# Two heads on one core: the first phase recorded, ordered by a list scheduler in the kernel, and its first keys loaded early

## The chip, the cores and the metric

The kernel runs on one core of a Trainium2 chip. The metric is the device time of one execution in microseconds (us). The engines are PE (TensorE, matrix products), DVE (VectorE), ACT (ScalarE), POOL (GpSimd) and SP (SyncE, which here only issues DMAs). Each takes its instructions in a fixed order; semaphores hold an instruction until what it reads is there and what it overwrites is free.

## The reference

Two independent heads share the sequence of 2048 positions; their outputs of 448 columns each are put side by side. Inputs and outputs are float32.

```python
# head A: a diagonal state-space convolution, 448 channels, 256 states each
dt = exp(log_dt); A = -exp(log_A_real) + 1j * A_imag; C = (C_real + 1j * C_imag) * dt[:, None]
P = exp((A * dt[:, None])[:, :, None] * pos)
K = 2.0 * einsum("dn,dnl->dl", C, P).real
y = irfft(rfft(u_t, 2 * L) * rfft(K, 2 * L))[:, :, :L]
a = y + u * D_skip
# head B: full attention, 16 heads of 28
q, k, v = split(x @ wqkv)
p = softmax(einsum("bhqd,bhkd->bhqk", q, k) * 28 ** -0.5)
b = einsum("bhqk,bhkd->bhqd", p, v) @ wo
out = concatenate([a, b], axis=-1)
```

## The kernel before

**Phases.** `body` has a first phase (the block `with ExitStack() as st:`) and a main loop behind it. The first phase computes queries, keys and values, the *seeds* (the exponentials from which the main loop multiplies up the powers of head A), and the largest scores of the first attention unit. The main loop runs over 16 units (4 groups of 4 heads by 4 chunks of 512 queries) of 16 key tiles each, and mixes scores, exponentials, products with v, the maxima of the next unit and head A's convolution by a written list of slots. Only the first phase is changed.

**Projections.** x comes in four chunks of 512 positions (`load_x`, tile `xn`), is transposed on PE and split into a high and a low part (`xh`, `xl`). `qk_proj(c, s, g)` multiplies chunk c with the weights of group g (s = 1 for keys, 0 for queries): 12 matmuls of 512 columns into a PSUM bank `pm`; ACT and DVE evict it into `hl`, and SP stores it to DRAM (`k_d`, `q_d`). `v_proj` does the values with 12 matmuls of 448 columns; they go to `v_d`. For half of the keys a difference is stored as well (`dhl`, `kd_d`). That makes 48 jobs in the list `work`; in the last chunk the four value jobs stand ahead of the eight others.

**Seeds.** `seeds(o)` handles one of eight octets of channels: loads (`nat`), scales on ACT, transposes into `pn`, phases and sizes in the large tile `tri`, sines and exponentials on ACT (which needs another function table for each kind), products on POOL and DVE (`qhat` as a workspace, `sg`, `px`), and two stores into `sd_d`. The octets are interleaved with the projections in steps: octet o starts its stages at step `SP * o`, and `PW = 37` steps hold the 48 projection jobs.

**First maxima.** Softmax needs an upper bound of each row's scores. For unit 0 it is found at the end of the first phase: 16 groups (4 heads by 4 tiles of 128 queries) of five matmuls. The maximum of two blocks of scores is built as relu(a - b) + b: a product of the query with the key difference `kdif` (or with one quarter of the keys, less another, by means of the negated queries `nq`) goes through ACT's relu into `rl`, and one DVE instruction adds b and reduces. Both halves of a group share tiles of two banks, so there are 16 relus of 1024 columns and 16 reductions of 1024. `max_end` transposes the 16 columns and `max_put` writes the negated maxima `mh` into two rows of the queries `qhat`, by a DMA on ACT's queue. Only then can the main loop's scores `pss` start.

**Places.** The keys of group 0 lie in `k0_t`. The same memory holds the split weights of the projections until these are done:

```python
        w_g = k0_t[:CK].rearrange("p g (i s k h e) -> p i s k g h e", i=2, s=2, k=NCK, h=HG)
```

so the key loads, written at the steps `KW = (33, 35, 36)` and behind step `PW`, wait for the last projection that reads the weights of that head. The maxima have their own pools (`m_p`, `ps_2`), opened when the projections' pools are closed.

**Order.** `KEPT["p"] = ()` leaves the first phase to the framework's own scheduler, which sets the order of instructions on each engine when the kernel is built; `KEPT["a"]` keeps the main loop's engines in the order of the program. `project` emits an eviction one job later than its matmuls.

Of the kernel before, what the change touches and what calls it, by code (L numbers as in the profile page):

```python
# [8 lines left out]
F32 = mybir.dt.float32  # L9
F32R = mybir.dt.float32r  # L10
# [7 lines left out]
L = 2048  # L18
# [25 lines left out]
A0, A1, KW = 26, 34, (33, 35, 36)  # L44
# [21 lines left out]
class Kept:  # L66
# [5 lines left out]
    def __getattr__(self, name):  # L72
        f = getattr(self.engine, name)

        def call(*args, **kw):
            i = f(*args, **kw)  # L76
            return self.owner.tc.keep_in_program_order(i) if self.name in self.owner.kept else i
        return call


class Engines:
    def __init__(self, tc):
        self.tc, self.kept = tc, ()
        for n in ("tensor", "vector", "scalar", "gpsimd", "sync"):
            setattr(self, n, Kept(self, n, getattr(tc.nc, n)))


KEPT = {"p": (), "a": ("tensor", "vector", "scalar", "gpsimd", "sync"), "f": ()}
# [3 lines left out]
def body(ctx, tc, a, out):  # L92
# [41 lines left out]
    k0_p = pool(k0_st, "k0_p", side="right")  # L134
    k0_t = k0_p.tile([128, HG, L], F32R, name="khat")
# [10 lines left out]
    def load_k(g, j, p):  # L146
        if j == 0:
            t = k0_t if g == 0 else p.tile([128, HG, L], F32R, name="khat")
            kt_g[g] = [t[:, i] for i in range(HG)]
        for r in range(4):  # L150
            nc.sync.dma_start(kt_g[g][j][32 * r:32 * r + 32, :].bitcast(F32), k_d[g][r % 2, 32 * j:32 * j + 32, :])
# [47 lines left out]
    def max_end(u, ps):  # L199
        nc.tensor.transpose(ps[:16, :128], m_u[u, 1], ident)  # L200
        mh = q_p.tile([16, 2, 128], F32R, name="mh")
        nc.vector.tensor_scalar(mh[:, 0, :], ps[:16, :128], -1.0, None, op0=ALU.mult)
        nc.vector.scalar_tensor_tensor(mh[:, 1, :], ps[:16, :128], -1.0, mh[:, 0, :].bitcast(F32),
                                       op0=ALU.mult, op1=ALU.subtract)
        mh_u[u] = mh
# [7 lines left out]
    with ExitStack() as st:  # L213
        sst, xst, wst, mst, psx, psm = (ExitStack() for _ in range(6))
# [3 lines left out]
        y_p = pool(wst, "y_p", side="right")  # L218
        ps_w[0] = pool(psx, "ps_w", 1, PSUM)
# [3 lines left out]

        xns = {}

        def load_x(c):
            xs = x[c * CQ:(c + 1) * CQ, :].rearrange("(t p) d -> p t d", p=128)
            for h in range(2):
                xns[c, h] = y_p.tile([128, 2, D], F32, name="xn", bufs=3)
                nc.sync.dma_start(xns[c, h], xs[:, 2 * h:2 * h + 2, :])  # L230

        load_x(0)
        w_g = k0_t[:CK].rearrange("p g (i s k h e) -> p i s k g h e", i=2, s=2, k=NCK, h=HG)
        vh = y_p.tile([CK, NCK, D], F32R, name="vh")
        vl = y_p.tile([CK, NCK, D], F32R, name="vl")
        nc.gpsimd.memset(k0_t[:CK].rearrange("p g (n e) -> p (g n) e", e=32)[:, :, DH:].bitcast(F32), 0.0)
        vst = [v_p.tile([128, NK // NQ, HG, 32], F32, name="v", bufs=5).rearrange("p t h e -> p (t h) e") for _ in range(2)]
        for t in vst:
            nc.gpsimd.memset(t[:, :, DH:DH + 1], 1.0)
            nc.gpsimd.memset(t[:, :, DH + 1:], 0.0)  # L240
        wns = []
        for i in range(2):
            wn = t_p.tile([128, 3, LV, BO * 16], F32, name="tri", bufs=2).rearrange("p t k h -> p (t k h)")
            wn = wn[:CK, :2 * 3 * D].rearrange("p (k s d) -> p k s d", k=2, s=3)
            wns += [wn[:, 0], wn[:, 1]]
# [7 lines left out]
        def load_nat(o):  # L253
            nats[o] = s_p.tile([PO, 4, 256], F32, name="nat", bufs=2)
            for i, n in enumerate(("A_log_A_real", "A_A_imag", "A_C_real", "A_C_imag")):
                nc.sync.dma_start(nats[o][:, i, :], bass.AP(tensor=a[n].tensor, offset=a[n].offset + first(o) * 256,
                                                            ap=[[256, JF // 4], [JF * 256, 4], [1, 256]]))
# [47 lines left out]
        def turn_dt():  # L305
            dt_ps = ps_t.tile([128, CQ], F32, name="pt")[:PO, :NO]
            nc.tensor.transpose(dt_ps, dt_o, ident[:NO, :NO])
            for i, f in enumerate((1.0, 0.15915494309189535, 2.0, -2.0, -1.0)):
                nc.vector.tensor_scalar(dt_all[:, i, :], dt_ps, f, None, op0=ALU.mult)
# [4 lines left out]
        def seeds(o):  # L314
# [13 lines left out]
            def turn():  # L328
                pn = ps_n.tile([128, CQ], F32, name="pn")
                q["ps"] = ps = pn[:, :8 * PO].rearrange("p (a b h e) -> p a b h e", a=4, h=2, e=8)  # L330
                q["magic"] = pn[:, 8 * PO:8 * PO + 1]
                vec.tensor_scalar(q["magic"], half_pi, 0.0, MAGIC, op0=ALU.mult, op1=ALU.add)
                for i in range(4):
                    for h in range(2):
                        nc.tensor.transpose(ps[:, i, :, h, :], q["nat"][:, i, h * 128:(h + 1) * 128], ident[:PO, :PO])
                q["tr"] = s_p.tile([128, NH], F32, name="tr", bufs=2)
                act.activation(q["tr"], ps[:, 0].rearrange("p b h e -> p (b h e)"), AF.Copy)

            def phases():
                tri = t_p.tile([128, 3, LV, NH], F32, name="tri", bufs=2)  # L340
# [14 lines left out]
            def places():  # L355
                se = q_p.tile([128, HG, CQ], F32R, name="qhat", bufs=3).bitcast(F32).rearrange("p h q -> p (h q)")
# [5 lines left out]
            def g_place():  # L362
                q["sg"] = sg = s_p.tile([128, BO, SDF - F_G], F32, name="sg", bufs=SGB)
# [36 lines left out]
            def g_first():  # L400

                c0 = q["ps"][:, 2:4].rearrange("p c b h e -> p c (b h e)")
                px = ps_x.tile([128, CQ], F32, name="px")
# [29 lines left out]
        def transposes(c):  # L433
            for k in range(NCK):
                pt = ps_t.tile([128, CQ], F32, name="pt")[:CK]
                for t in range(4):
                    nc.tensor.transpose(pt[:, t * 128:(t + 1) * 128], xns[c, t // 2][:, t % 2, k * CK:(k + 1) * CK], ident)
                xh[k] = x_p.tile([CK, CQ], F32R, name="xh", bufs=XB)
                xl[k] = x_p.tile([CK, CQ], F32R, name="xl", bufs=XL)
# [3 lines left out]
        def qk_proj(c, s, g):  # L443
            pp = w_tile()
# [7 lines left out]
            def evac():  # L452
                hl = x_p.tile([128, 2, CQ], F32R, name="hl", bufs=2)
# [7 lines left out]
                if s == 1 and c < 2:  # L461
                    HC = CQ // 2
                    kb = y_p.tile([128, HC], F32, name="kb")
                    dhl = y_p.tile([128, 2, HC], F32R, name="dhl")
# [10 lines left out]
        def v_proj(c, t):  # L475
            pp = w_tile()
# [12 lines left out]

        work = []  # L490
        for c in range(NQ):
            jobs = [lambda c=c, s=s, g=g: qk_proj(c, s, g) for g in range(G) for s in (1, 0)]
            v_jobs = [lambda c=c, t=t: v_proj(c, t) for t in range(4)]
            jobs = v_jobs + jobs if c == NQ - 1 else jobs + v_jobs
# [11 lines left out]
        pend, n_work = [], len(work)  # L506
# [7 lines left out]
        for j, t in enumerate(KW):  # L514
            ahead[t].append(lambda j=j: load_k(0, j, k0_p))

        def project():

            e = work.pop(0)() if work else None
            while pend:  # L520
                pend.pop(0)()
            if e:
                pend.append(e)

        for t in range(n_stage):
            while work and n_work - len(work) < n_work * (t + 1) / PW:
                project()
            for f in slots[t] + ahead.get(t, []):
                f()
            if t + 1 == PW:  # L530
                project()
                wst.close()
                load_k(0, HG - 1, k0_p)
                load_q(1)
                for c in range(NQ):
                    load_v(0, c)
        xst.close()
        psx.close()
        m_p = pool(mst, "m_p")
        ps_2 = pool(psm, "ps_2", 4, PSUM)  # L540
        nq = m_p.tile([128, HG, CQ], F32R, name="nq")
        m_u[0, 1] = q_p.tile([128, HG * 4], F32, name="m1", bufs=2)
        for i in range(16):
            j, t = divmod(i, 4)
            ts = slice(t * 128, (t + 1) * 128)
            q, kt = q_u[0][:, j, ts], kt_g[0][j]
            if t == 0:
                nc.gpsimd.tensor_scalar(nq[:, j], q_u[0][:, j].bitcast(F32), -1.0, None, op0=ALU.mult)
            pd, pb = (ps_2.tile([128, 2, CQ], F32, name="p2") for _ in range(2))
            kb = kt.rearrange("p (c s n) -> p c s n", c=NQ, s=2)[:, :2, 1, :]  # L550
            mm = nc.tensor.matmul
            mm(pd[:, 0], q, kd_g[0, j], start=True, stop=True)
            mm(pd[:, 1], q, kt[:, 2 * CQ:3 * CQ], start=True, stop=False)
            mm(pd[:, 1], nq[:, j, ts], kt[:, 3 * CQ:], start=False, stop=True)
            mm(pb[:, 0].rearrange("p (c n) -> p c n", c=2), q, kb, start=True, stop=True)
            mm(pb[:, 1], q, kt[:, 3 * CQ:], start=True, stop=True)
            rl = m_p.tile([128, 2, CQ], F32, name="rl2", bufs=2)
            nc.scalar.activation(rl, pd, AF.Relu)
            nc.vector.tensor_tensor_reduce(rl, pb, rl, 1.0, -3.0e38, ALU.add, ALU.max, m_u[0, 1][:, i:i + 1])
        nc.scalar.activation(half_pi[:1], half_pi[:1], AF.Exp)  # L560
        max_end(0, ps_2.tile([128, 2, CQ], F32, name="p2")[:, 0])
        max_put(0)
        psm.close()
        mst.close()
# [12 lines left out]
    k_pools = [k0_p, kq_p]  # L577
# [580 lines left out]
```

## Time and profile before

| | |
|---|---|
| median of 3 runs | 1305.49 us (1304.11 to 1305.54) |
| profiled execution | 1307.74 us, of which the span of the trace is 1305.7 us |
| busy in the span | PE 1228.7 us (94%), ACT 980.3 (75%), DVE 907.0 (69%), POOL 865.9 (66%) |
| DMA | 205.28 MB, mean 157 GB/s |
| granted TensorE clock, mean | 0.976 |

All times below are of the one profiled execution. Busy shares are averages over phases with different limits, so they are read by stretches of time. A row of the timeline gives start, duration, engine, line, operation, target and sources, and in brackets how long the engine had been idle and what ended that. A row of a group gives the count, the busy time, the mean time of one in ns, and the idle time before them. Nearly all instructions carry line 76, the helper that passes every call on, so groups are told apart by the names of their tiles. SPq is SP issuing a DMA: its time is that of the issue, not of the transfer.

### The profile page before, as it was taken

How to read it: one execution, taken by the hardware profiler on the slowest of the kernel's cores; microseconds unless marked ns; L12 is line 12 of the kernel's file. 1: busy time of each engine (PE TensorE's matmuls, PEld its weight loads, DVE VectorE, ACT ScalarE, POOL GpSimd, SP SyncE). 2: the span in 40 equal slices, each digit the busy share in tenths (PEclk: the TensorE clock that was granted, in tenths of full speed). 3: DMA queues.
4: the chain of work that ended last, by engine and by line, in shares of the span. 5: the costliest groups of instructions: out<-in, count | busy, mean ns of one | idle time of the engine just before them, and what ended most of it. 6: DMA issues, size and time to landing. Idle time of an engine off the chain costs nothing.

```text
span 1305.7 us, 32148 instructions
## 1 busy us (share of the span) xinstructions
PE 1228.7 (94%) x12193; PEld 695.7 (53%) x12193; DVE 907.0 (69%) x2001; ACT 980.3 (75%) x2046; POOL 865.9 (66%) x684
## 2 busy tenths in 40 slices
PE   6888877799999999999999999999997999999998
PEld 5766755355555555555555555555554555545333
DVE  5676656677777787777788888888986555636111
ACT  4877875588888888888788888888886666756463
POOL 2677654478888788888769999999995221424421
PEclk9989887799999999999999999999999999999999
DMA  6677679735866455468634232743324453647666
GB/s 202 207 273 257 218 259 271 212 66 136 185 147 142 109 149 157 142 169 231 162 104 105 56 83 62 157 111 78 82 59 139 146 158 136 203 142 238 202 161 175
DMA packets 200082, 205.28 MB, mean 157 GB/s; under 512 B 95992, under 2 KB 158520, under 8 KB 197880
## 3 DMA queue, kind: packets, MB, share of 16 engines
q1 hardware_dynamic: 199864, 203.22, 56.1%
q8 instruction: 96, 1.57, 0.5%
q14 instruction: 58, 0.48, 0.1%
q10 hardware_dynamic: 64, 0.02, 0.0%
HBM read 120.74 MB, written 82.18 MB: 155 GB/s over the span
## 4 chain that ended last, share of the span: by engine, by line
PE 72%; POOL 8%; ACT 7%; DVE 5%; DMA 4%; issue 4%; SPq 0%; ACTq 0%; POOLq 0%
PE pm L76 39%; PE pss L76 16%; PE po L76 16%; POOL sg L76 2%; POOL e L76 2%; DMA khat<-k 2%; POOL tri L76 2%; ACT tri L76 1%; ACT sg L76 1%; DVE mx L76 1%; POOL p L76 1%; ACT L76 1%; ACT p L76 1%; POOL eu L76 1%; DVE rl L76 1%
## 5 line engine op out<-in xcount | busy, mean ns | idle before, releaser
L76 ACT ACTIVATE p<-pss 128x512 f32<-128x512 f32 x1024 | 560.4, 609 | 109.9 <-PE pss L76 105.9
L76 PE MATMUL pss<-qhat,khat 128*128 128x512 f32 x1024 | 405.7, 402 | 4.0 <-DMA qhat<-mh 2.2
L76 DVE TENSOR_REDUCE mx<-pm 128x1 f32<-128x512 f32 x480 | 308.3, 683 | 121.2 <-PE pm L76 119.5
L76 PE MATMUL pm<-khat,qhat 128*128 128x512 f32 x720 | 314.4, 437 | 6.1 <-ACT rl L76 3.5
L76 POOL TENSOR_TENSOR e<-e,sdb 128x256 f32<-128x256 f32 x168 | 202.0, 1203 | 108.7 <-ACT e L76 67.2
L76 PE MATMUL po<-p,v 128*32 128x512 f32 x2048 | 271.0, 597 | 0.0
L76 POOL TENSOR_TENSOR e<-e,eu 128x256 f32<-128x256 f32 x168 | 248.3, 1478 | 13.2
L76 PEld LDWEIGHTS pm<-khat,qhat 128*128 128x128 f32 x720 | 135.4, 188 | 206.4 <-ACT p L76 47.0
L76 PEld LDWEIGHTS pss<-qhat,khat 128*128 128x128 f32 x1024 | 191.2, 189 | 52.5 <-ACT p L76 13.8
L76 DVE CUSTOM_DVE_ANT_0 rl<-pm,rl 128x512 f32<-128x512 f32 x240 | 165.3, 689 | 70.0 <-ACT rl L76 67.7
L76 POOL TENSOR_TENSOR eu<-e,sdb 128x256 f32<-128x256 f32 x168 | 202.3, 1204 | 0.0
L76 POOL TENSOR_TENSOR p<-pr,pr 64x448 f32<-64x448 f32 x64 | 73.2, 1144 | 155.6 <-PE pm L76 122.3
L76 DVE TENSOR_TENSOR g<-g,zg 128x128 f32<-128x128 f32 x392 | 162.0, 413 | 3.6
L76 ACT ACTIVATE rl<-pm 128x512 f32<-128x512 f32 x240 | 145.3, 605 | 7.7 <-issue 4.1
L76 PE MATMUL pm<-xh,khat 112*128 112x512 f32 x256 | 89.7, 431 | 19.6 <-DVE hl L76 10.6
L76 PE MATMUL pm<-kdif,qhat 128*128 128x512 f32 x240 | 97.0, 404 | 1.7 <-DVE pr L76 1.1
L76 DVE TENSOR_TENSOR zg<-g,zg 128x128 f32<-128x128 f32 x224 | 88.0, 393 | 5.3
L76 PEld LDWEIGHTS pm<-e,g 128*32 128x32 f32 x3584 | 56.9, 110 | 49.2 <-issue 15.7
L76 PE MATMUL pm<-e,g 128*32 128x64 f32 x3584 | 73.6, 223 | 8.7 <-POOL e L76 8.7
L76 ACT ACTIVATE y<-pm 128x448 f32<-128x448 f32 x48 | 26.5, 553 | 59.7 <-PE pm L76 39.1
L76 PEld LDWEIGHTS pm<-xh,khat 112*128 112x128 f32 x256 | 51.0, 205 | 35.9 <-DVE hl L76 12.6
L76 DVE TENSOR_TENSOR pr<-pm,ub 128x448 f32<-128x448 f32 x64 | 37.0, 619 | 46.9 <-PE pm L76 37.7
(133 smaller groups left out, 1491.6 us busy)
## 6 DMA issues: line engine op xcount, KB each, us to landing
sdb<-sd SPq DMA_DIRECT2D x56, 336.0 KB
khat<-k SPq DMA_DIRECT2D x64, 256.0 KB
qhat<-q SPq DMA_DIRECT2D x64, 256.0 KB
sd<-sg SPq DMA_DIRECT2D x8, 1456.0 KB
k<-hl SPq DMA_DIRECT2D x16, 512.0 KB
q<-hl SPq DMA_DIRECT2D x16, 512.0 KB
v<-v SPq DMA_DIRECT2D x32, 256.0 KB
mw<-in_mw SPq DMA_DIRECT2D x16, 512.0 KB
```

The costliest lines, as they stand in the source:

```text
L76: i = f(*args, **kw)
```

## The change

Every instruction of the first phase is recorded instead of issued, with what it reads and writes. `Plan.order` gives each a duration from a table or a formula, builds the dependences from overlapping memory, and lays the instructions on five engines and one DMA resource by list scheduling: at each step the engine that is free first takes the ready instruction with the longest remaining chain. Then they are issued in that order, and all five engines are kept in it. Tiles that the framework rotated are now rings made ahead (`ring`), so that reuse is seen as a dependence.

The weights get a place of their own (`w_p`). The keys' place is opened when the chunks of x and the values' weights are done with (`change`), which needs the last value job done; the value jobs of the last chunk therefore stand second to fifth in it. From job 41 on, `first_maxima` asks for the keys of heads 2, 3, 0 and 1 and records the groups of maxima in the jobs' order (`MG`: job number to head of keys, groups). Each group is done in two halves of one bank each, from the projections' own rings: 32 relus and 32 reductions of 512 columns in place of 16 of 1024. The negated queries use the place of `nat`; three of the four `xl` tiles use the places of `v`. An eviction is recorded with its job. The differences and queries of group 0 are asked for at steps 18 and 28 (before 26 and 34); the next queries and the values are loaded through the plan.

```diff
-A0, A1, KW = 26, 34, (33, 35, 36)
+A0, A1 = 18, 28
+MG = {41: (2, ()), 42: (3, ()), 43: (0, (8, 9)), 44: (1, (10, 11)), 45: (None, (12, 13)), 46: (None, (14, 15)), 47: (None, (0, 1)),
+      48: (None, (2, 3)), 49: (None, (4, 5)), 50: (None, (6, 7))}
...
+            if self.owner.plan is not None:
+                return self.owner.plan.add(self.name, name, lambda *a_, **k_: self.owner.tc.keep_in_program_order(f(*a_, **k_)), args, kw)
...
+    def order(self):
...
+        cost = lambda o: o.span + o.wait + (2.5 + o.bytes / o.rate if o.bytes else 0.0)
+        for o in reversed(self.ops):
+            k = o.tag, o.engine
+            tail[o.i] = max([cost(o) + self.GAP + tail[j] for j in after[o.i]] + [o.span + chain.get(k, 0.0), cost(o)])
+            chain[k] = tail[o.i] if o.engine != "sync" else 0.0
...
+        while len(out) < n:
+            e = min((e for e in pools if pools[e]), key=lambda e: max(free[e], min(ready[i] for i in pools[e])))
+            t = max(free[e], min(ready[i] for i in pools[e]))
+            best = max((i for i in pools[e] if ready[i] <= t + 1e-9),
+                       key=lambda i: tail[i] * self.SCALE[self.ops[i].tag] + self.BIAS[self.ops[i].tag] - (0 if self.ops[i].table in (None, table[0]) else self.SWITCH))
...
+            if o.bytes:
+                dma[0] = max(dma[0], end + 1.3) + o.bytes / o.rate
+                end = dma[0] + 0.6
...
-KEPT = {"p": (), "a": ("tensor", "vector", "scalar", "gpsimd", "sync"), "f": ()}
+KEPT = {"p": ("tensor", "vector", "scalar", "gpsimd", "sync"), "a": ("tensor", "vector", "scalar", "gpsimd", "sync"), "f": ()}
...
-        w_g = k0_t[:CK].rearrange("p g (i s k h e) -> p i s k g h e", i=2, s=2, k=NCK, h=HG)
+        w_t = w_p.tile([CK, HG, L], F32R, name="w")
+        w_g = w_t.rearrange("p g (i s k h e) -> p i s k g h e", i=2, s=2, k=NCK, h=HG)
...
+        def change():
+            yst.close()
+            k0.append(pool(k0_st, "k0_p", side="right"))
+            t = k0[0].tile([128, HG, L], F32R, name="khat")
+            kt_g[0] = [t[:, i] for i in range(HG)]
...
+        def max_group(i):
...
+            for h in range(2):
+                pd, pb = pt_r(), pm_r()
+                if h == 0:
+                    mm(pd, q, kd_g[0, j], start=True, stop=True)
+                    mm(pb.rearrange("p (c n) -> p c n", c=2), q,
+                       k_late(j, CQ, lambda t_: t_.rearrange("p (c s n) -> p c s n", c=NQ, s=2)[:, :2, 1, :]), start=True, stop=True)
+                else:
+                    mm(pd, q, quarter(2), start=True, stop=False)
+                    mm(pd, Late(("nq", j), 128, lambda: nqs[j][:, ts]), quarter(3), start=False, stop=True)
+                    mm(pb, q, quarter(3), start=True, stop=True)
+                rl = rl_r()
+                nc.scalar.activation(rl, pd, AF.Relu)
+                nc.vector.tensor_tensor_reduce(rl, pb, rl, 1.0, -3.0e38, ALU.add, ALU.max, m_u[0][:, j, t, h:h + 1])
...
-            jobs = v_jobs + jobs if c == NQ - 1 else jobs + v_jobs
+            jobs = jobs[:1] + v_jobs + jobs[1:] if c == NQ - 1 else jobs + v_jobs
...
+        plan.do("sync", 2.0, 1 << 20, lambda: load_q(1), [], [se_r()])
+        for c in range(NQ):
+            plan.do("sync", 0.5, 1 << 18, lambda c=c: load_v(0, c), [], [(vst + xls)[c]])
+        nc.plan = None
+        plan.run()
...
-        for i in range(16):
-            j, t = divmod(i, 4)
...
-            rl = m_p.tile([128, 2, CQ], F32, name="rl2", bufs=2)
-            nc.scalar.activation(rl, pd, AF.Relu)
-            nc.vector.tensor_tensor_reduce(rl, pb, rl, 1.0, -3.0e38, ALU.add, ALU.max, m_u[0, 1][:, i:i + 1])
```

## What was predicted before the run

> **What bounds the kernel now.** I read the page first, then the stretches, then the end of the first phase in order of time. The stretches show two kernels in one.
>
> ```profile
> span 1305.7 us, 32148 instructions
> 0.00:160.00 160.00, 132.97 (x585) 104.35 (x586) 105.89 (x175) 114.17 (x204) 94.86 (x83) 0.95 0.70 230
> 10.00:180.00 170.00, 149.53 (x661) 117.64 (x661) 117.15 (x189) 126.82 (x224) 106.97 (x74) 0.95 0.71 237
> 190.00:240.00 50.00, 34.20 (x111) 22.99 (x110) 27.51 (x50) 29.39 (x37) 15.50 (x12) 0.80 1.05 290
> 300.00:1305.00 1005.00, 982.44 (x10916) 521.35 (x10915) 710.24 (x1649) 774.27 (x1683) 690.05 (x543) 1.00 0.53 140
> ```
>
> After the stretch come busy us of PE, PEld, DVE, ACT and POOL, then granted clock, DMA share and GB/s. From 300 us on PE is busy 982.44 of 1005 us, and every engine's instructions there are the same rows in the same order in both kernels. So a microsecond won or lost before the first real scores reaches the end whole, and nothing else can change. In the first phase no compute engine is full: from 10 to 180 us PE is at 88%, ACT at 75%, DVE at 69%. From 190 to 240 us the DMA engines are full (1.05) and PE idles a third of the time. The end of the phase, row by row:
>
> ```profile
> 191.94 2.69 SPq L76 DMA_DIRECT2D khat<-k  x4
> 207.49 0.79 PE L76 MATMUL p<-kdif,qhat 128*128 128x512 f32 x1 [7.14 <-DVE hl L76]
> 233.82 0.37 SPq L76 DMA_DIRECT2D sd<-sg  x1
> 235.57 0.08 DVE L76 DVE_READ_ACCUMULATOR2_ANT m<- 128x1 f32 x1
> 236.38 2.10 ACTq L76 DMA_DIRECT2D qhat<-mh  x2
> 236.38 5.56 DMA qhat<-mh
> 242.00 1.28 SPq L76 DMA_DIRECT2D sdb<-sd  x3
> 245.15 0.63 ACT L76 ACTIVATE e<-sdb 128x256 f32<-128x256 f32 x1 [6.02 <-DMA sdb<-sd]
> 246.36 1.08 ACT L76 ACTIVATE p<-pss 128x512 f32<-128x512 f32 x2
> ```
>
> The keys are asked for at 191.94; the first maximum starts at 207.49, after the last projection has been evicted; the last one is read at 235.65; the shifts `mh` land in `qhat` at 241.94. The seeds of block 0 (`sdb`) are asked for only at 242.00, since SP waits there behind the last seed store, and land at 245.15. ACT stands at them, ahead of the first `p`, until 246.36. That instant is the phase's end in what follows. Some 28 us of it are maxima with nothing beside them.
>
> **The change, part by part.** First the keys and maxima move. In PE's rows the first operand of a name is the target: `p`/`pt` and `pm` are PSUM banks, `kdif`, `khat`, `nq`/`nat` the operands of a maximum, `xh`, `xl`, `w` those of a projection. Before, at the end of the projections:
>
> ```order
> L76 MATMUL pm_1744<-xl,khat 128x512
> L76 MATMUL pm_1744<-xh,khat 128x512 x2
> L76 MATMUL pm_1744<-xl,khat 128x512
> L76 MATMUL p_1823<-kdif_1373,qhat 128x512
> L76 MATMUL p_1823<-khat,qhat 128x512
> L76 MATMUL p_1824<-khat,qhat 128x512 x2
> ```
>
> Now, in the last quarter of the tokens, with seven of its projections still to come:
>
> ```order
> L79 MATMUL pm<-xl,w 128x512
> L79 MATMUL pt<-kdif_205,qhat 128x512
> L79 MATMUL pn<-ident,nat 128x7x8 x6
> L79 MATMUL pt<-kdif_205,qhat 128x512
> L79 MATMUL pn<-ident,nat 128x7x8 x2
> L79 MATMUL pm<-khat,qhat 128x512
> L79 MATMUL pt<-khat,qhat 128x512
> L79 MATMUL pt<-khat,nat 128x512
> L79 MATMUL pm<-khat,qhat 128x512 x3
> L79 MATMUL pt<-khat,qhat 128x512
> L79 MATMUL pt<-khat,nat 128x512
> L79 MATMUL pt<-kdif_205,qhat 128x512
> ```
>
> Ten of the 16 groups of maxima now stand between projections, six behind the last. On SP's queue (`k_57` the stored keys of group 0, `sd_85` to `sd_88` seed stores of the last octets, `q_3` and `k_58` stores of projections), before:
>
> ```order
> L76 DMA sd_87<-qhat 128x7x256
> L76 DMA kdif_1634<-kd_61 32x512 x2
> L76 DMA khat<-k_57 32x2048 x4
> L76 DMA k_59<-hl 128x2x512
> L76 DMA qhat<-q_0_65 32x4x512 x2
> ```
>
> and now:
>
> ```order
> L79 DMA khat<-k_57 32x2048
> L79 DMA v_97<-v 512x1x128 x2
> L79 DMA khat<-k_57 32x2048 x10
> L79 DMA q_3_68<-hl 128x2x512
> L79 DMA k_58<-hl 128x2x512
> L79 DMA khat<-k_57 32x2048
> L79 DMA sd_86<-qhat 128x7x256
> ```
>
> The first key load goes past three stores of projections (`q_3_68`, `k_58`, `q_3_72`) and three of seeds (both of `sd_86`, the first of `sd_87`).
>
> *When the keys can start, T.* They need the values of the last quarter done, since their buffer lies where x and the values' weights were. Ahead of that point PE's new order has 605 matmuls. Before, PE had started 585 at 160 us, and 20 more at the spacing below make 164.6.
>
> ```profile
> 213.40 0.63 PE L76 MATMUL p<-khat,qhat 128*128 128x512 f32 x1
> 213.83 0.63 PE L76 MATMUL p<-khat,nq 128*128 128x512 f32 x1
> 217.31 0.40 PE L76 MATMUL p<-khat,qhat 128*128 128x512 f32 x1
> 217.54 0.39 PE L76 MATMUL p<-khat,nq 128*128 128x512 f32 x1
> L76 ACT ACT_TABLE_LOAD x17 | 21.8, 1283 | 1.0 <-PEq L1148 0.7
> L76 ACT ACTIVATE rl<-p 128x1024 f32<-128x1024 f32 x16 | 16.3, 1026 | 10.9 <-PE p L76 10.4
> L76 ACT ACTIVATE rl<-pm 128x512 f32<-128x512 f32 x240 | 145.3, 605 | 7.7 <-issue 4.1
> ```
>
> PE idled 20.5 of the 170 us from 10 to 180. Of this I give the new order a third back, 7 us (bounds: none, and 15; an order can also lose, see the rivals), so T = 158. The table loads fall from 17 to 13 by the order, 4 x 1.283 = 5.1 us of ACT; the maxima in halves cost ACT 32 x 0.605 - 16 x 1.026 = 2.9 us more. ACT's list is thus 2.2 us shorter, nothing by itself.
>
> *From T to the last maximum.* PE has 84 matmuls of projections and 80 of maxima, 164 x 0.23 = 38 us. DVE has the longest list that PE waits for:
>
> ```profile
> L76 DVE TENSOR_TENSOR tri<-tri 128x1680 f32<-128x1680 f32 x8 | 21.1, 2640 | 0.1
> L76 DVE CUSTOM_DVE_ANT_0 rl<-p,rl 128x1024 f32<-128x1024 f32 x16 | 19.2, 1224 | 8.3 <-ACT rl L76 7.8
> L76 DVE CUSTOM_DVE_ANT_0 rl<-pm,rl 128x512 f32<-128x512 f32 x240 | 165.3, 689 | 70.0 <-ACT rl L76 67.7
> L76 DVE TENSOR_TENSOR tri<-pn,pw 128x1680 f32<-128x1680 f32 x8 | 15.2, 1905 | 0.2
> L76 DVE SCALAR_TENSOR_TENSOR tri<-tri,pn 128x1680 f32<-128x1680 f32 x8 | 15.2, 1900 | 0.1
> L76 DVE SCALAR_TENSOR_TENSOR hl<-pm,kones,hl 128x512 fp32r<-128x512 f32 x16 | 11.9, 744 | 16.4 <-ACT hl L76 16.2
> L76 DVE TENSOR_TENSOR hl<-pm,hl 128x512 fp32r<-128x512 f32 x16 | 11.0, 687 | 11.4 <-ACT hl L76 11.2
> L76 DVE TENSOR_TENSOR sg<-sg,px 128x224 f32<-128x224 f32 x16 | 9.0, 562 | 0.2
> ```
>
> 32 x (0.689 + 0.08) = 24.6 for maxima (3.7 more than 16 x (1.224 + 0.08)); 3 x 0.744 + 4 x 0.687 = 5.0 for projections; 2 x 1.900 + 2 x 2.640 + 1.905 = 11.0 and 18 small ones of at most 0.562, 10.1, for seeds: 50.7 us. At DVE's 69% from 10 to 180 us that is 73.5 us, unbroken 50.7. I take 80%, 63.4 us: above the 69% because a third independent stream, the maxima, can fill its waits, well below 100% because the seeds still hop between DVE, POOL and ACT. So the last maximum is read at 158 + 63.4 = 221.4 (235.65 before), `mh` lands 6.3 later at 227.7, and the first `p` follows about 1.2 later (as 245.15 to 246.36): 228.9.
>
> *The DMA engines.* Behind the first key load stand, by the order: 16 khat, 3 k, 4 q, 4 qhat, 6 v, 3 + 3 sd.
>
> ```profile
> sd<-sg SPq DMA_DIRECT2D x8, 1456.0 KB
> k<-hl SPq DMA_DIRECT2D x16, 512.0 KB
> q<-hl SPq DMA_DIRECT2D x16, 512.0 KB
> sd<-qhat SPq DMA_DIRECT2D x8, 896.0 KB
> v<-v SPq DMA_DIRECT2D x20, 256.0 KB
> khat<-k SPq DMA_DIRECT2D x16, 256.0 KB
> qhat<-q SPq DMA_DIRECT2D x12, 256.0 KB
> ```
>
> That is 17296 KB, 17.7 MB, at 290 GB/s 61.1 us: `sdb` is asked for at 219.1 and lands 3.2 later, 222.3, before `mh`. The transfers just fit; they hide behind DVE by 5 us, and with that cover gone they set the end.
>
> *Added waits.* PE now stops at the first matmul on the early keys, seven projections behind it. Four loads and two v stores, 1.57 MB or 5.4 us, face 24 matmuls, 5.5 us, so 0 to 3 us are lost. The first q store stands behind eleven key loads, up to 2.9 MB or 10 us; its `hl` buffer is needed for a later eviction, which PE waits for in turn: 0 to 4 us. Both lie inside the span from 50.7 to 73.5.
>
> So the first `p` comes at 228.9, not 246.4: 17.4 us less. The profiled execution took 1307.74 us (span 1305.7), the median of the three runs is 1305.49. I forecast 1305.5 - 17.4 = 1288 for the median.
>
> [...] The row from 190 to 240 us has the clock at 0.80 where PE idles, and matmuls stand 0.43 us apart at 213.40 against 0.23 later. At 0.43 throughout, 164 matmuls take 70.5 us; the end would come 7 us later, near 1295. [...] The trace shows both spacings.
>
> **The rivals.**
> *The engines keep their pace* (DVE at 69%): 158 + 73.5 + 7.5 = 239.0, 7.4 us less, 1298. For it: the seeds' hops are not shortened. Against: from 10 to 180 us no maxima were there to fill them.
> *More is recovered.* T = 150 and DVE at 90%, 56.3 us, end the maxima path at 213.8; the transfers then end last, 150 + 61.1 + 3.2 + 1.2 = 215.5, 30.9 us less, 1275.
> *The held order costs T.* Slower: ahead of T each seed alternates between engines.
>
> ```profile
> DVE sg L76 <- POOL tri L76: 23.2, 7, 5.5
> ACT tri L76 <- POOL tri L76: 21.4, 11, 3.7
> ```
>
> 18 such waits of 2.5 us on average, about 11 of them before T (five of eight octets). A planned duration that is off lengthens them, and evictions of projections stand behind on DVE and ACT, so PE follows. It decides from T = 175.5 (175.5 + 63.4 + 7.5 = 246.4), 10.9 us later than before's own pace: 1.0 us per wait. At 1.6 us each T is 182.2 and the time 1312. Against it: both kernels issue in a fixed order, and the new one is made from spans for these shapes. [...]
> *It does not do what it says*: the order shows the maxima between the projections, so this is left only as keys that land too late, which is the first rival.
>
> **How the numbers follow.** Forecast 1288: 0.55. Pace kept or PE slow in its pauses, 1298 and 1295: 0.17. More recovered, 1275: 0.11. Held order slower, 1312: 0.14. The pieces cancel: 0.03. A measurement tells 0.2% (2.6 us) from no change, so faster 0.83, same 0.03, slower 0.14. The range reaches from 1273, below the transfers' bound by 2, to 1303, the kept pace with T five later; it leaves out the slower cases and the tails, about 0.2.
>
> **What would show it.** Right: keys asked for at 155 to 162, the first maximum some 8 us later, a last maximum near 221, the first `p` near 229, DMA share near 1 from T to 220, DVE near 80% there, 13 table loads. Pace kept: DVE at 69% and the first `p` at 239. Wrong: keys asked for after 175, or PE idle in the last quarter of the tokens with waits on `hl` or `khat` of over 10 us, or a main loop that lasts longer than before.

## The result, and the profile after

The changed kernel takes 1286.32 us (median of 4 runs, 1282.35 to 1289.8), the kernel before 1305.47 in the same comparison (1304.11 to 1305.54): a ratio of 0.9855, interval 0.9825 to 0.9885. The forecast was 1288. The profiled execution took 1287.11 us, its span is 1285.2. First the stretches, in the columns used above (busy us and instructions of PE, PEld, DVE, ACT and POOL; granted clock, DMA share, GB/s):

```profile
0.00:160.00 160.00, 138.49 (x616) 110.29 (x616) 107.05 (x176) 115.17 (x202) 91.18 (x80) 0.96 0.79 260
157.40:222.70 65.30, 55.57 (x180) 35.99 (x179) 49.88 (x110) 48.36 (x85) 43.04 (x29) 0.84 0.90 266
157.40:190.00 32.60, 27.00 (x89) 18.30 (x88) 25.36 (x43) 22.59 (x41) 27.06 (x17) 0.79 0.99 269
190.00:222.70 32.70, 28.57 (x92) 17.68 (x91) 24.51 (x67) 25.76 (x45) 15.98 (x13) 0.90 0.80 264
190.00:240.00 50.00, 43.67 (x141) 25.79 (x140) 36.68 (x96) 36.62 (x66) 28.94 (x25) 0.83 0.78 238
```

PE has started 616 matmuls by 160 us (585 before), and from 190 to 240 us it is busy for 43.67 us (34.20 before). The end of the phase, from the timeline:

```profile
157.42 0.34 SPq L79 DMA_DIRECT2D khat<-k  x1
169.61 0.40 PE L79 MATMUL pt<-kdif,qhat 128*128 128x512 f32 x1
218.80 0.37 SPq L79 DMA_DIRECT2D sd<-sg  x1
219.22 8.64 SPq L80 DMA_DIRECT2D sdb<-sd  x3
222.62 0.08 DVE L79 DVE_READ_ACCUMULATOR2_ANT mx<- 128x1 f32 x1
225.84 0.65 ACT L80 ACTIVATE e<-sdb 128x256 f32<-128x256 f32 x1 [0.16 <-DMA sdb<-sd]
228.68 0.60 ACT L80 ACTIVATE p<-pss 128x512 f32<-128x512 f32 x1 [0.79 <-PE pss L80]
```

and the transfer of `mh` from the chain of waits:

```profile
224.49 3.25 DMA qhat<-mh
```

The keys are asked for at 157.42 (191.94 before), the last maximum is read at 222.70 (235.65), and the first `p` starts at 228.68 (246.36): 17.7 us earlier. The span is 20.5 us shorter. The other 2.8 us lie in the main loop, where both kernels have the same rows and the forecast expected no difference; from the first `p` to the end the twelve traces below and this one take 1056.1 to 1058.5 us, the trace of before 1059.3. The waits of the first 208 us, before and then after (waiting engine and tile, releaser, us in total, times, longest):

```profile
DVE hl L76 <- ACT hl L76: 27.5, 14, 5.3
PEld pm L76 <- DVE hl L76: 17.3, 7, 5.7
PE pm L76 <- DVE hl L76: 14.5, 7, 5.2
```

```profile
DVE hl L79 <- ACT hl L79: 13.7, 11, 3.9
PEld pm L79 <- DVE hl L79: 7.9, 5, 2.6
```

Before, PE's matmuls stood 14.5 us, and its weight loads 17.3 us, for banks whose eviction DVE had not finished. Now the loads stand 7.9 us, and the matmuls 6.3. DVE's wait for ACT's part of the eviction is halved.

### The profile page after: what moved, and what is told of

Its sections match the earlier page's. It is cut to its first block, busy times and chain, and to the rows that moved or that the text cites. A ratio compares the mean times of both kernels' runs of the same rounds, so it can differ in the third digit from the quotient of the medians.

```text
span 1285.2 us, 32244 instructions
## 1 busy us (share of the span) xinstructions
PE 1229.8 (96%) x12193; PEld 695.9 (54%) x12193; DVE 910.9 (71%) x2034; ACT 979.7 (76%) x2058; POOL 867.4 (67%) x684
## 4 chain that ended last, share of the span: by engine, by line
PE 78%; DVE 7%; POOL 5%; issue 4%; ACT 4%; DMA 2%; SPq 0%; ACTq 0%; POOLq 0%; DVEq 0%
PE pm L80 39%; PE pss L80 17%; PE po L80 16%; PE pm L79 6%; POOL e L80 2%; DVE mx L80 1%; POOL p L80 1%; DMA tri<-in_B_wqkv 1%; POOL eu L80 1%; DVE sg L79 1%; ACT p L80 1%; DVE rl L79 1%; DVE px L79 1%; DMA q<-hl 1%; DVE tri L79 1%
## 5 line engine op out<-in xcount | busy, mean ns | idle before, releaser
L79 PE MATMUL pm<-xh,w 112*128 112x512 f32 x256 | 90.4, 438 | 5.4 <-DVE hl L79 2.0
L80 PEld LDWEIGHTS po<-p,v 128*32 128x32 f32 x2048 | 54.4, 110 | 26.2 <-issue 21.6
```

The costliest lines, as they stand in the source:

```text
L79: return self.owner.plan.add(self.name, name, lambda *a_, **k_: self.owner.tc.keep_in_program_order(f(*a_, **k_)), args, kw)
```

## The experiments

All twelve start from the changed kernel; the kernel before ran beside them at 1303.3 to 1304.6 us. Six of the times form a table (ratios to the kernel before, with their intervals):

| order of the first phase | keys late, maxima last | keys early, maxima beside projections |
|---|---|---|
| the framework's | 1317.72 (1.0104, 1.0087 to 1.0121) | 1332.54 (1.022, 1.0204 to 1.0235) |
| planned, table switches penalised (the change) | 1287.8 (0.9879, 0.9865 to 0.9894) | 1286.32 (0.9855, 0.9825 to 0.9885) |
| planned, no penalty | 1287.73 (0.9878, 0.9857 to 0.9898) | 1274.63 (0.9771, 0.9753 to 0.9788) |

The penalty is the 10 us that the plan takes off the remaining chain of an ACT instruction which needs another function table than the one loaded.

**Late keys, planned order.** The theory of the prediction was that maxima beside the projections fill DVE's waits; the rival, that the order alone gains.

```diff
-MG = {41: (2, ()), 42: (3, ()), 43: (0, (8, 9)), ...
+MG = {48: (2, ()), 49: (3, ()), 50: (0, ()), 51: (1, ())}
-        y_all = [xn_r(), xn_r(), xn_r(), vh, vl, kb_t, dhl_t]
+        y_all = [xn_r(), xn_r(), xn_r(), vh, vl, kb_t, dhl_t, w_t]
```

> List order kept, but the keys' place also waits for the projections' weights, and keys and maxima are recorded behind the last projection: the order part of the change alone. Theory (the order gives a smaller part, the maxima beside the projections the larger): projections end near 200 us, the first maximum near 207, 16 groups at DVE's 1.54 us each to 232, first p near 239.5, time 1298 (1293 to 1302). Rival 1 (the order alone carries the gain): 1289 or less. Rival 2 (the order is worth nothing by itself): 1305.

1287.8 us: the rival. From its waits, and from its timeline (the last projection, the first `p`):

```profile
PE pm L78 <- DMA khat<-k: 11.7, 1, 11.7
```

```profile
183.35 0.63 PE L78 MATMUL pm<-xl,w 112*128 112x512 f32 x1
228.39 0.60 ACT L79 ACTIVATE p<-pss 128x512 f32<-128x512 f32 x1 [2.00 <-PE pss L79]
```

The projections end at 184, PE then waits 11.7 us for keys, and yet the first `p` comes at 228.39, as with early keys. "Late" holds for 13 of the 16 key loads (from 187.84 on) and for every product with the keys (from 195.72 on); three loads still went out between 151.91 and 171.21. DVE was busy for 50.83 of the 65.0 us from 157.4 to 222.4 here, 78%.

**Early keys, framework's order.** The recording is issued as it was written, and the framework's scheduler sets the order.

```diff
...
-        for i in self.order():
-            self.ops[i].run()
+        for o in self.ops:
+            o.run()
...
-KEPT = {"p": ("tensor", "vector", "scalar", "gpsimd", "sync"), ...
+KEPT = {"p": (), ...
```

> Early keys and halved maxima as in the change, but the first phase is issued as recorded and the framework's scheduler sets the order again: the other part alone. Theory (both parts needed): T back near 165, DVE at 69 to 76% behind it, first p at 236 to 244, time 1294 to 1303. Rival 1 (early keys alone carry the gain): 1289 or less. Rival 2 (early keys without a planned order gain nothing): 1305 or more.

1332.54 us, slower than before, the second rival: in its timeline the keys are asked for at 183.13 and the seeds at 267.36, 48 us later than in the changed kernel.

```profile
183.13 1.97 SPq L172 DMA_DIRECT2D khat<-k  x4
267.36 1.37 SPq L80 DMA_DIRECT2D sdb<-sd  x3
273.34 1.08 ACT L80 ACTIVATE p<-pss 128x512 f32<-128x512 f32 x2
```

**Late keys, framework's order.** Both edits together.

> The framework's order, as in the run that took 1332.5, but with the keys asked for behind the last projection and all maxima behind them: of the change only the rings, the halves and the new places are left. If the early keys are what made that run slow (they hold two PSUM rings and the key place while projections wait), this one comes back to the kernel before, 1303 to 1312. If the fixed rings and the order of the recording made it slow, it stays at 1325 to 1340. I take the first, near 1308: the maxima in halves cost DVE 3.7 and ACT 2.9 us more, and nothing of it is hidden behind projections.

1317.72 us, 14 slower than before and above the 1303 to 1312 that I took. So early keys cost this order another 15 us, and rings, halves and new places cost it 14; what each of these three costs was not taken apart.

**Half of the maxima.** The second half of each group is not issued, so the bound covers half of the keys.

```diff
+                if h:
+                    for o in plan.ops[n_ops:]:
+                        o.run = lambda: None
-... rearrange("p a b c -> p (a b) c")[:, :, :2], ...
+... rearrange("p a b c -> p (a b) c")[:, :, :1], ...
```

> Same order as the change, but the second half of each of the 16 groups of maxima isn't issued (48 matmuls, 16 relus, 16 reductions; the bound then covers half of the keys): 12.3 us off DVE behind T. Theory (from T on DVE's list sets the maxima's end, but the seed path ends only 3 us ahead of it): the first p is then held by the first seeds, 224 to 227 instead of 228.7, time 1281 to 1285. Rival 1 (DVE's list sets both ends): 12.3 / 0.76 = 16 us off, 1270. Rival 2 (transfers set the end): unchanged, 1286.

1279.74 us (0.9806, 0.9788 to 0.9825). The end of its phase in the timeline:

```profile
213.65 1.72 ACTq L79 DMA_DIRECT2D qhat<-mh  x2
216.17 1.28 SPq L80 DMA_DIRECT2D sdb<-sd  x3
219.03 0.65 ACT L80 ACTIVATE e<-sdb 128x256 f32<-128x256 f32 x1 [3.02 <-DMA sdb<-sd]
```

ACT now waits 3.02 us for `sdb`: the seed loads are the bound, as expected (the time is a little below the 1281 to 1285 given), but not the work on the seeds. The last seed store went out at 208.80; SP's queue then stood 6.9 us until `mh` had landed (213.65 + 2.51 = 216.16), and only then asked for `sdb`. The end moves only 8.4 us, and 4.0 of these lie ahead of the keys (asked for at 153.44, not 157.42), where nothing was taken out. Behind the keys `mh` lands 7.6 us earlier, and 4.4 of these reach the first `p`.

**More transfers.** The three last `sg` stores are made twice, 4.47 MB more.

```diff
+                    plan.ops[-1].run = lambda: (first_run(), keep(dma(sx_d[o][:, :, F_G:] ..., q["sg"])))
```

> Same order, but the larger seed store of each of the last three octets is issued a second time to a spare place: 4.47 MB more behind T, 15.4 us at 290 GB/s. Theory (transfers are full from T to 190 us only and hide behind the engines after that): the first seeds land 3 to 5 us later, behind the last extra store, first p near 232, time 1288 to 1291. Rival (the transfers set the end): 1302.

1289.66 us (0.9888, 0.987 to 0.9907), within the expected 1288 to 1291 and far from the 1302 of the rival. In its trace the keys are asked for at 152.49, 4.9 us earlier than in the changed kernel, with the same order of PE up to there, and the last maximum is read 65.8 us later (65.3 in the changed kernel). The seed loads are asked for at 224.30, and ACT waits for them:

```profile
227.43 0.63 ACT L80 ACTIVATE e<-sdb 128x256 f32<-128x256 f32 x1 [5.50 <-DMA sdb<-sd]
```

The expectation had the loads wait behind the last extra store; the trace shows another wait. SP sent that store at 214.80 and then stood 8.9 us until `mh` had landed (219.27 + 5.01 = 224.28). So the extra transfers don't set the end of the maxima; what they would do to the seed loads alone, this run doesn't tell.

**The recorded order, held.** The list scheduler is left out, the engines are still held.

```diff
-        for i in self.order():
-            self.ops[i].run()
+        for o in self.ops:
+            o.run()
```

> The list scheduler is left out: the instructions are issued in the order in which they were recorded, and all five engines are held in that order. Early keys, halves and rings stay. If holding any fixed order is what gains, the time stays near 1286 to 1292. If the planned order is what gains, the recorded order does no better than the framework's order of the same recording, which took 1332.5: 1315 to 1345, with long waits of DVE and ACT on POOL in the seeds and 17 table loads where the plan has 13 (5.1 us of ACT). I take the second.

1419.43 us (1.0889, 1.0873 to 1.0905), far beyond what either theory gave. By 160 us PE has started 346 matmuls (616 in the changed kernel), and no engine but PE is busy half of the time; below the stretch, the two longest waits of the first 220 us:

```profile
0.00:160.00 160.00, 83.71 (x346) 68.24 (x347) 64.88 (x119) 71.55 (x122) 51.20 (x50) 0.81 0.46 145
```

```profile
DVE hl L79 <- ACT hl L79: 69.7, 19, 8.4
PE pn L79 <- DVE pn L79: 63.0, 5, 19.2
```

Holding an order is no gain in itself: the same recording took 1332.54 where the framework set the order.

**Flat durations.**

```diff
+        o.span = o.span if o.bytes else 0.2 if engine == "tensor" else 0.8
```

> The list scheduler stays, but is told that every instruction of PE takes 0.2 us and every one of DVE, ACT and POOL 0.8 us, whatever its size; only the DMAs keep their durations. (In the trace those of DVE, ACT and POOL last from 0.2 to 3.1 us.) If the dependences and the longest remaining chain carry the plan, the time stays within 6 us of 1286. If the durations carry it, a seed's step of 1.9 to 3.1 us that the plan takes for 0.8 makes the engines behind it wait in order: eight octets with about six such hops at 0.5 to 1 us each are 24 to 48 us, of which PE's order hides half or more: 1300 to 1312, about what the rival of the held order gave. I take 1302.

1340.76 us (1.0274, 1.0254 to 1.0295). The keys are asked for 41.6 us later than in the changed kernel:

```profile
198.99 3.59 SPq L79 DMA_DIRECT2D khat<-k  x8
```

The loss is 54 us; I had priced it at 16.

**Formula durations.**

```diff
-    SPANS = {("gpsimd", "tensor_tensor", 784): 1.87, ...
+    SPANS = {}
```

> The plan's table of nine durations is emptied, so that the formulas by size alone serve: a POOL product of 1680 columns is planned at 4.4 us (3.1 in the changed kernel's trace), one of 784 at 2.16 (1.87), a DVE product of 1680 at 1.90 (2.58); the other sizes are off by less than 15%. If a plan needs its durations only coarsely, 1285 to 1292. If every tenth counts, the place is half way to the run with flat durations (1340.8): 1300 to 1315. I take the first, 1290.

1278.86 us (0.9803, 0.9784 to 0.9822): 7.5 us better than with the table, and below both expected ranges. The formula is worse for POOL's product of 1680 columns (4.4 us, 3.1 in the trace) and better for DVE's: it gives 1.90, the table 2.3, and six of the eight `tri<-tri` products of the changed kernel took 1.90 to 1.92. (The 2.58 of the expectation is a mean into which one of 6.84 us went; see the end.) With flat durations the plan loses, so coarse sizes are needed; that exact ones help is not shown.

**No preference for seeds.**

```diff
-    SCALE = {"p": 1.0, "s": 1.15, "m": 1.0, "d": 1.0}
+    SCALE = {"p": 1.0, "s": 1.0, "m": 1.0, "d": 1.0}
```

> The seeds' remaining chain counts as it is (factor 1.0) and no longer 1.15 times, when the plan chooses the next instruction. Durations and dependences are the same. The last seed store held the first seed load back in the changed kernel (218.80 to 219.22 us), and the maxima end 4 us later. If the longest remaining chain is all that a plan needs, 1284 to 1292. If the plan is only as good as its hand-set preference, the seeds come later, their long hops lie behind the projections instead of beside them, and DVE, ACT and POOL have them together with all maxima: 1300 to 1315. I take the second, 1303.

1310.13 us (1.0047, 1.0031 to 1.0062): 24 us lost by one number, the factor on the seeds' remaining chain. The first 100 us, in the changed kernel and here:

```profile
0.00:100.00 100.00, 86.15 (x387) 68.53 (x387) 64.66 (x115) 66.96 (x126) 49.37 (x51) 0.97 0.80 259
```

```profile
0.00:100.00 100.00, 85.02 (x383) 67.57 (x384) 47.95 (x88) 50.27 (x97) 28.36 (x35) 0.98 0.70 222
```

PE goes on as before, but DVE and POOL have done 17 and 21 us less of the seeds. As expected, these come behind.

**A warmer PE.**

```diff
+                if t > 140 and self.begin[i] - t > 0.5:
+                    for _ in range(int((self.begin[i] - t) / 0.15)):
+                        self.fill()
```

> The changed kernel, with 83 spare transposes of 64 columns into a corner of px that nothing reads, put in PE's order at 13 places of the last quarter where the plan leaves PE idle. In the changed kernel's trace the granted clock was 0.66, 0.76, 0.90 and 0.66 in the four stretches of 10 us from 160 to 200 us, where PE was busy for 33.0 us. If that clock is what eats the overlap, it rises to 0.9 or more there, PE's 33 us shrink by up to a quarter, 8 us, and the time falls to 1279 to 1283, held then by the seeds as in the run with half of the maxima (1279.7). If the hops between DVE, ACT and POOL set the pace, the clock rises and the time stays at 1285 to 1288. If the spare work stands in the way (83 at 0.12 us are 10 us of PE, where its real waits are elsewhere than the plan has them), 1289 to 1296. I take the second.

1286.87 us (0.9868, 0.9843 to 0.9893). The stretch from 160 to 200 us, in the changed kernel and here:

```profile
160.00:200.00 40.00, 32.97 (x99) 22.69 (x99) 30.42 (x55) 27.08 (x47) 33.29 (x21) 0.74 0.99 289
```

```profile
160.00:200.00 40.00, 34.02 (x166) 24.21 (x166) 31.36 (x58) 28.61 (x51) 35.95 (x24) 0.88 0.97 281
```

The granted clock rose from 0.74 to 0.88, and PE was busy for 1.05 us more. Of its 166 matmuls 63 are spare ones (5.68 us), so its own 103 took 28.3 us, where 99 took 33.0; and the time stayed. The higher clock by itself brought nothing that the runs can tell (1286.87 and 1286.32). In the trace of the changed kernel the pace changes in the middle of unbroken work: after several waits of up to 1.3 us, PE works from 194.38 on with matmuls 0.42 us apart, and only behind 199.2, 4.8 us later, do they come at 0.23.

```profile
194.38 1.22 PE L79 MATMUL pm<-xh,w 112*128 112x512 f32 x2 [0.27 <-DVE mx L79]
198.38 0.95 PE L79 MATMUL pm<-xh,w 112*128 112x512 f32 x2
199.18 0.39 PE L79 MATMUL pm<-xl,w 112*128 112x512 f32 x1
199.40 0.40 PE L79 MATMUL pt<-kdif,qhat 128*128 128x512 f32 x1
```

**No penalty for table switches.**

```diff
-    SWITCH = 10.0
+    SWITCH = 0.0
```

> The plan no longer avoids changes of ACT's function table (SWITCH = 0 where it was 10), so it has 17 table loads, as the kernel before, and not 13. Four loads of 1.283 us are 5.1 us of ACT. If they lie on the path of the first phase, 1290 to 1293. If they fall into ACT's waits (ACT is busy 115.2 of the first 160 us in the changed kernel), as the prediction had it, 1284 to 1289. I take the second.

1274.63 us (0.9771, 0.9753 to 0.9788), with 17 table loads: 11.7 us faster than the changed kernel, below both cases of the expectation, and the best version of the study. The changed kernel's timeline at the place where the difference is plainest (`pn` is the transposed `nat` of an octet, `v` the eviction of the values):

```profile
147.77 0.27 PE L79 MATMUL pn<-ident,nat 56*128 56x56 f32 x1
153.51 0.95 ACT L79 ACTIVATE v<-pm 128x448 f32<-128x448 f32 x2
154.48 1.28 ACT L79 ACT_TABLE_LOAD   x1
155.78 0.77 ACT L79 ACTIVATE sg<-tri 128x672 f32<-128x672 f32 x1
157.02 0.37 PE L79 MATMUL pm<-vh,xl 112*128 112x448 f32 x1
157.79 0.39 PE L79 MATMUL pn<-ident,nat 56*128 56x56 f32 x3
158.22 0.28 DVE L79 TENSOR_SCALAR tri<-pn 128x112 f32<-128x112 f32 x1 [8.32 <-PE pn L79]
```

and without the penalty, the same step and the phase's end, then the stretch:

```profile
147.65 0.51 PE L79 MATMUL pn<-ident,nat 56*128 56x56 f32 x5
148.20 0.28 DVE L79 TENSOR_SCALAR tri<-pn 128x112 f32<-128x112 f32 x1 [3.95 <-PE pn L79]
152.83 0.34 SPq L79 DMA_DIRECT2D khat<-k  x1
216.21 0.59 ACT L80 ACTIVATE p<-pss 128x512 f32<-128x512 f32 x1
```

```profile
160.00:200.00 40.00, 33.02 (x120) 21.64 (x119) 29.50 (x68) 37.40 (x58) 33.07 (x24) 0.96 1.05 316
```

With the penalty most of an octet's transposes stand behind the value projections in PE's order (the last of these is the row at 157.02), and DVE waits 8.32 us for them. Without it they stand ahead, at 147.65. The keys are asked for 4.6 us earlier, and from there to the first `p` it takes 63.4 us, not 71.3. The 4.6 us are not shown to come from the penalty: the traces with half of the maxima (153.44) and with more transfers (152.49) have it too. Behind the keys, the other traces with the penalty and all maxima took 70.1 us (warmer PE) and 76.2 (more transfers). ACT is busy for 37.40 of the 40 us from 160 to 200, where the penalty left it at 27.08. The load at 154.48 starts 0.02 us after its predecessor ends and takes 1.28 us, and ACT's next instruction starts 0.02 us behind it. How the penalty leads to that order of PE is not shown, only that it does.

**Late keys, no penalty.** The last run asks whether the overlap is worth something under the better order.

> The late keys of the run that took 1287.8 (keys asked for behind the last projection, all maxima behind them), with the plan's penalty for a change of function table at 0, as in the run that took 1274.6. If the maxima's place beside the projections is worth nothing, whatever the plan, and the order of the seeds is all, this one takes 1272 to 1278. If the overlap is worth something once the rest of the order doesn't spoil it, it stays behind the early keys by what the overlap saves: 1280 to 1288. I take the second, 1284: with late keys PE waited 11.7 us for the keys and the maxima ran by themselves at the end, and with the penalty at 0 the early keys had a granted clock of 0.96 from 160 to 200 us, where the run with the penalty had 0.74.

1287.73 us (0.9878, 0.9857 to 0.9898), as late keys with the penalty. So without the penalty the early keys and maxima are worth 13.1 us; with it 1.5, which its runs cannot tell from nothing. What joins the two, so that the early keys pay only without the penalty, is not shown.

## Why the prediction was right

*The keys' start, T.* Forecast 158, measured 157.42. The time given back is there, and the waits on `hl` show from where. That it was a third of PE's idle time is in part luck: with the same order of PE up to there, three other traces have

```profile
153.44 0.34 SPq L79 DMA_DIRECT2D khat<-k  x1
152.49 0.34 SPq L79 DMA_DIRECT2D khat<-k  x1
159.79 0.34 SPq L79 DMA_DIRECT2D khat<-k  x1
```

(half of the maxima, more transfers, the warmer PE). The order alone gives back more than a third in the first two.

*DVE's list.* Forecast 50.7 us at 80%, read at 221.4. Measured 49.88 us in 65.30, 76%, read at 222.70. `mh` landed 5.0 us later (224.49 + 3.25 = 227.74), not 6.3: its transfer took 3.25 us, at a DMA share of 0.51, where before it had taken 5.56, at 0.85. The differences cancel, and the first `p` came at 228.68 (forecast 228.9); that it fits to 0.2 us is luck, since each of the terms is off by 0.3 to 1.9 us. In the list of 50.7 us, 2 x 2.640 was a mean pulled up by two products of over 4 us; behind the keys the two took 1.90 us each.

*The reason for the 80%* fell, and it is the step that failed: maxima as a third stream that fills DVE's waits beside the projections. With late keys no product with the keys runs beside a projection, and yet DVE is busy 78% of the same stretch (76% with early keys) and the phase ends at the same time. So in the changed kernel that stream brings 1.5 us of 19. The planned order brings the rest (the framework's order of the same late keys takes 1317.72, 30 us more), and the waits for evictions are shorter in it. The overlap is real (13.1 us) only in the order without the penalty.

*The transfers.* `sdb` was asked for at 219.22 (forecast 219.1), for another reason. After 190 us the DMA share is 0.80, so the 61.1 us of transfers were not what held it. SP stood 4.5 us at the last seed store (218.80), which waits for the seeds. The loads landed at 225.84, not 222.3, and hid 1.9 us behind `mh`, not 5. The reading of the kernel before was wrong here: the loads at 242.00 did not wait behind the last seed store (233.82) but for `mh`, which landed at 241.94. SP's queue, before and after (what it waited for, us, times, longest):

```profile
SPq L76 <- DMA qhat<-mh: 7.7, 1, 7.7
SPq L80 <- DMA qhat<-mh: 6.6, 1, 6.6
```

In the changed kernel two of the three loads go out ahead of that wait (219.22 and 219.89), and the third behind it (227.55, about when `mh` lands). So from `mh` to the first `p` it takes 0.9 us and not 4.4, which is 3.5 of the 17.7 us won. The forecast has this step (1.2 us), but takes it from the sum of the transfers.

*The added waits.* PE's wait for the early keys is not in the list of waits at all (0 of 0 to 3 us), nor is a wait for the stores that free `hl` behind the keys' start (0 of 0 to 4). ACT does wait for such stores, 3.9 us for keys and 1.1 for queries, but between 26 and 36 us.

*The table loads* were called "nothing by itself". The loads themselves seem to be: the run without the penalty has four more and is faster. But avoiding them cost 11.7 us, through the order, a cost that the forecast left out.

*The rivals.* The held order that costs T is a real mechanism, with a price too low: 1.6 us per wait gave 1312, where flat durations take 1340.8 and an unplanned order 1419.4. The chance of 0.14 was for this plan, which was good enough to keep T. PE's low clock (1295) is in the rows (0.79 from 157.4 to 190 us), with no pause of PE over 1.82 us there; but raising the clock (0.74 to 0.88 from 160 to 200 us) brought nothing. The time of the case of 1275 was reached by another kernel: 1274.63 without the penalty, with T at 152.8. Its bound was not: from T to the first seed load that kernel took 55.3 us, not the 61.1 of the transfers (which ran at 316 GB/s from 160 to 200 us, not at 290).

## What to carry to other kernels

When engines are held in a planned order, cost the order apart from the overlap that it is meant to allow: run the same plan with the overlap taken away, and the same overlap without the plan. A plan's weights and penalties are guesses; try each at its neutral value, since one number here was worth 12 us and another 24. Ask each DMA queue for its own waits: here the seed loads stood behind a transfer that they don't need. Durations had to be right in their coarse sizes; finer ones were not shown to help.

## What was not expected of the hardware

The changed kernel's runs spread over 7.5 us (1282.35 to 1289.8), and those with the spare transposes as much (1282.86 to 1290.28), where the other experiments spread over 1.1 to 5.8 and the kernel before over 1.4 to 4.6. The traces show one place where such a difference arises. In the changed kernel's trace, ahead of the keys:

```profile
133.99 6.84 DVE L79 TENSOR_TENSOR tri<-tri 128x1680 f32<-128x1680 f32 x1
139.15 3.43 POOL L79 TENSOR_SCALAR sg<-sg 128x672 f32<-128x672 f32 x1
```

The same DVE product took 2.15 us with more transfers, 2.00 with half of the maxima and 3.37 with the spare transposes; the POOL instruction took 1.89 with more transfers. POOL was at work almost without a pause from 130.89 to 142.58, and behind DVE's product PE stood 3.20 us (at 141.49). It is most of the 4.9 us by which the keys came later than with more transfers. That the two engines held each other up there, which the plan's durations don't know, is a guess: no run took POOL's work away, so that is not shown. With late keys and no penalty another such product took 5.60 us (at 174.39). The trace with the spare transposes was already behind at 100 us, ahead of the first of them (369 matmuls started, 387 in the changed kernel), so this is not the only such place.

The issue of the three `sdb` loads took SP 8.64 us in the changed kernel and 1.28 before. What holds it is the wait for `mh` above. It falls ahead of the first load before, with half of the maxima and with more transfers, behind the first without the penalty, behind the second in the changed kernel, and behind all three with late keys. No seed load reads `mh`; why SP must wait for it, and what moves the place of the wait, is not in the traces.
